# The first attention block by 64-key tiles in eight steps, and the second x tile normalised on Pool

## The chip, the cores and the metric

The kernel runs on one core of a Trainium2 chip. The metric is the device time of one execution in microseconds (us). The core has a matrix engine (TensorE, PE in the profile, its weight loads PEld), VectorE (DVE), ScalarE (ACT), GpSimd (Pool) and a queue engine that issues transfers (SyncE, SP). Each runs its own instructions in the order in which they stand, and waits for the others by semaphores. Matrix results land in PSUM, here in banks of 128 x 512 float32; in this kernel VectorE and ScalarE move them on, never Pool.

## What is computed

S = 2048 rows, D = 448 columns, 16 heads of 28, a window W of 256 keys, a feed-forward width F = 1792. The two branches read the same normalised x, and everything is summed:

```python
q, k, v = qkv[0], qkv[1], qkv[2]          # xn @ wqkv
scores = jnp.einsum("bhqd,bhkd->bhqk", q, k) * (Dh ** -0.5)
mask = (idx[:, None] - idx[None, :] >= 0) & (idx[:, None] - idx[None, :] < W)
p = _softmax(jnp.where(mask[None, None], scores, -1e9), axis=-1)
A = (p @ v) @ wo
B = (_gelu(xn @ w_gate) * (xn @ w_up)) @ w_down
return x + A + B                           # xn = _layernorm(x)
```

## The kernel before

**Blocks.** The rows are worked in four blocks of 512 (`qb`). Each block has an attention stage, a gate stage (gate and up projections, Gelu, product) and a down projection that runs as filler in the next block's attention. One block's attention is a fixed list of score steps (`steps_of`): each step fills one PSUM tile `sc` of 128 keys x 4 heads x 512 columns (four banks), ScalarE takes its exponential into an SBUF tile `p_sb` (L688), the entries outside the window are zeroed, and later `pv` multiplies with V. There is only one `sc` tile in the attention stage, so a step's matmuls wait for the exponential of the step before. Between two steps TensorE is given filler work by a table, `plan`: a tuple `(u, 2)` takes two pieces from generator `u`, a function is called at its place, and strings such as "sums" name small jobs.

**Groups.** The 16 heads are four groups `g` of four heads. Queries and keys of a group come from `qk_copies`, V from `v_copy`. In the first block groups 1 to 3 are projected during steps 0 to 2 (`gen_qk`), then come the up projections of five of the seven column pairs (`gen_up`, tile `ue`), then V and the first three groups of the second block (`gen_pairs`, generator `w`).

**First block, before.** Keys go by tiles of 128: nine steps (L570 to L580), each of 8 matmuls of 28 x 128 weights. Pool zeroes the entries outside the window (`masked`, L614). A group's product with V uses one PSUM bank; VectorE copies it to `oc` (L666).

**Other blocks.** Keys go by tiles of 64, so that two halves of TensorE's rows work on two key tiles at once: 16 or 24 matmuls a step. VectorE multiplies the edges by ready-made masks (`apply_masks`, L604, three products a step). A group's product with V uses two banks, one for each half; ScalarE copies the first to `oc` (L640) and VectorE adds the second (`add_halves`, L641).

**Banks.** Four banks, b0 to b3, serve all work but the scores; `take` hands out the one that was given back longest ago and `give` returns one. A bank is free only when the engine that empties it has got to that copy in its own order. In the first block the second up projection takes the banks of the third group's query and key, which ScalarE (L243) and VectorE (L244) empty.

**After the V product**, `sums` transposes `oc` and takes reciprocals (VectorE), `inverse` spreads them (VectorE), `scale_o` multiplies on Pool (L623).

**Start.** x tiles 0 to 3 each pass statistics (`stat`, VectorE), `rstd` (two small ScalarE operations), `norm` (VectorE, L170), four transposes on TensorE and a copy out of PSUM (L186). Tiles 0 and 2 use bank b2, 1 and 3 bank b3. Tiles 4 to 7 are normalised during steps 0 and 2 (L170 again, two operations each) and transposed by DMA.

**SP's order** around step 2: transposes of tiles 5 to 7, the half-swapped copies `xsw` of tiles 4 to 7 (L469), the half-swapped weights `wsq` (L475), which wait for Pool's pad copies (`fill_pads`, L283 and L285), then the gate weights and the rest.

Of the kernel before, what the change touches and what calls it, by code (L numbers as in the profile page):

```python
# [10 lines left out]
ALU = mybir.AluOpType  # L11
# [6 lines left out]
P = 128  # L18
# [9 lines left out]
def kernel(  # L28
# [11 lines left out]
    nc = tc.nc  # L40
# [123 lines left out]

    def norm(t):
        xn = work.tile([P, 4, P], bf16, name="xn", bufs=4)
        xf = xn[:, :, :].rearrange("p a b -> p (a b)")
        both = ((0, D, 0), (D, 64, 384))
        for lo, n, src in both if t > 3 else both[:1]:
            nc.vector.tensor_scalar(out=xf[:, lo:lo + n], in0=x_sb[:, t, src:src + n], scalar1=mv_all[:, t, 0:1],  # L170
                                    scalar2=rstd_all[:, t:t + 1], op0=ALU.subtract, op1=ALU.mult)
        xns[t] = xn
# [336 lines left out]
    def gated(qb, early, last_v, flush, hook):  # L509
# [11 lines left out]
        def gate(p):  # L521
            gt = phase[0].pool.tile([P, 2, QB], f32, name="gt", tag="s")
            for c in range(7):
                chunk([gt[:, i, :] for i in range(2)], wg, p, qb, c)
            if not p:
                last_v()
            ges[p] = work.tile([P, 4, QB], bf16, name="p_sb", bufs=5)[:, 0:2, :]
            nc.scalar.activation(out=ges[p][:, :, :], in_=gt[:, :, :], func=ACT.Gelu_apprx_tanh)  # L528

        def end(p):  # L530
# [28 lines left out]
    def steps_of(qb):  # L559
# [6 lines left out]
        if not qb:  # L566
            def four(g):
                return [(g, None, 3, 384, 128, 0), (g, None, 0, 0, 384, 128)], 512, [(None, (0,), 2 * P, True), (None, (384,), P, False)]

            for g in (0, 2):  # L570
                yield four(g)
                if not g:
                    yield [(0, None, 1, 128, 384, 0), (0, None, 2, 256, 128, 384)], 512, [(None, (0, 384), P, True), (None, (256,), P, False)]
                    yield [(0, None, 2, 384, 128, 0), (1, None, 0, 0, 384, 128)], 512, [(None, (128,), P, True), (None, (384,), P, False)]
                    yield [(1, None, 3, 384, 128, 0), (1, None, 1, 128, 384, 128)], 512, [(None, (0,), 2 * P, True), (None, (384,), P, False)]
                    yield [(1, None, 2, 256, 256, 0), (2, None, 2, 256, 256, 256)], 512, [(None, (0, 256), P, True)]
                else:
                    yield [(2, None, 1, 128, 384, 0), (3, None, 3, 384, 128, 384)], 512, [(None, (0, 384), P, True), (None, (256,), P, False)]
                    yield [(3, None, 0, 0, 384, 0), (3, None, 2, 384, 128, 384)], 512, [(None, (0,), P, True), (None, (256,), P, False)]
                    yield [(3, None, 1, 128, 384, 0), (3, None, 2, 256, 128, 384)], 512, [(None, (0, 384), P, True), (None, (256,), P, False)]  # L580
            return
# [23 lines left out]

    def masked(p_sb, half, cols, w, diag):
        r = slice(0, P) if half is None else slice(64 * half, 64 * half + 64)
        for c in cols:
            reg = p_sb[r, :, c:c + w]
            mid = [[0, 4]]  # L610
            if w > P:
                reg = reg.rearrange("p h (b q) -> p h b q", q=P)
                mid.append([0, w // P])
            nc.gpsimd.affine_select(out=reg, in_=reg, pattern=mid + [[1 if diag else -1, min(w, P)]], compare_op=ALU.is_ge, fill=0.0,  # L614
                                    base=0 if diag else -1, channel_multiplier=-1 if diag else 1)

    def attention(qb, plan):
# [21 lines left out]
        def add_halves(oc, ov):  # L639
            nc.scalar.copy(out=oc[:, :], in_=ov[0][:, :])  # L640
            nc.vector.tensor_tensor(out=oc[:, :], in0=oc[:, :], in1=ov[1][:, :], op=ALU.add)  # L641
            give(*ov)
# [5 lines left out]
        def pv(g):  # L648

            ov = [take("ov") for _ in range(2 if qb else 1)]  # L650
            todo = parts.pop(g)
            for n, (half, kt, q0, nq, col, p_sb) in enumerate(todo):
                k0 = 64 * half if half else 0
                r = slice(k0, k0 + (P if half is None else 64))
                for j in range(4):
                    nc.tensor.matmul(ov[half or 0][32 * j:32 * j + 32, q0:q0 + nq], lhsT=v_sb[r, kt, 4 * g + j, :],  # L656
                                     rhs=p_sb[r, j, col:col + nq], start=n == (half or 0), stop=n + len(ov) >= len(todo),
                                     tile_position=(k0, 32 * j), skip_group_check=True)
            oc = work.tile([P, QB], f32, name="oc", tag="wb" if g % 2 else "wa", bufs=1)
            if qb:  # L660
                if g > 2:
                    behind.append((oc, ov))
                else:
# [8 lines left out]
        for i, (scores, ncol, edges) in enumerate(steps):  # L672
# [7 lines left out]
            for g, half, kt, q0, nq, col in scores:  # L680
                k0, nk = (64 * half, 64) if half is not None else (0, P)
                for j in range(4):
# [3 lines left out]
                                     tile_position=(32 * j, k0), skip_group_check=True)  # L686
                parts.setdefault(g, []).append((half, kt, q0, nq, col, p_sb))
            nc.scalar.activation(out=p_sb[:, :, 0:ncol], in_=ss[:, :, 0:ncol], func=ACT.Exp, scale=SCALE)  # L688
# [24 lines left out]
        def rest():  # L713
            while fresh:
                apply_masks(*fresh.pop(0))
            while later:
                scale_o(*later.pop(0))
            pv(2)
            pv(3)

        def after(f):
            if qb == NB - 1:
                if inverses:
# [41 lines left out]
    norm(2)  # L765
    transp(2, nc.scalar.copy, "b2")
# [45 lines left out]
    def ahead3():  # L812
# [19 lines left out]
    for qb in range(NB):  # L832
# [226 lines left out]
```

## Time and profile before

| what | value |
|---|---|
| median of 3 runs | 212.53 us (212.52 to 212.82) |
| the profiled execution | 212.69 us |
| its span in the profile | 210.8 us |
| granted TensorE clock over the span | full |
| first score step begins (PE) | 11.2 us |
| first gate matmul of block 0 (PE) | 37.15 us |
| first score step of block 1 (PE) | 51.9 us |

A row of the chain of waits has a start, a length and what ran. A row of the timeline has a start and a length (of all merged instructions, with xcount), the engine, the line, the operation and its output and inputs; in brackets the idle time before it and what ended that. A row of the costliest groups has busy time and mean length in ns of one, then the idle time before. Lines are those of the kernel before.

### The profile page before, as it was taken

The page shows a single profiled execution, that of the slowest core. Times are in us where ns is not written, and L with a number is a line of the kernel's source. Part 1 is how long each engine was busy: PE and PEld are TensorE (multiplying, and loading weights), DVE is VectorE, ACT ScalarE, POOL GpSimd, SP SyncE. Part 2 cuts the span into 40 slices and gives each one's busy share as a digit, 9 for nine tenths or more (in the row PEclk, how much of TensorE's full clock was granted, in tenths as well). Part 3 has the DMA queues.
Part 4 walks back from the last instruction along what each step waited for, and adds up shares of the span by engine and source line. Part 5 has one row for each costly group of instructions (what it writes and reads, how often), then busy time and mean ns, then how long its engine had stood idle before and what let it go on. Part 6 is the DMA issues. An engine that isn't in the chain of part 4 may idle for free.

```text
span 210.8 us, 6335 instructions
## 1 busy us (share of the span) xinstructions
PE 205.1 (97%) x2678; PEld 96.5 (46%) x2682; DVE 157.8 (75%) x356; ACT 132.0 (63%) x124; POOL 48.4 (23%) x83
## 2 busy tenths in 40 slices
PE   7899999999999999999999999999999999999994
PEld 2333444444444445444445444544444454544562
DVE  6899998999788985696438897395385699659722
ACT  4699588566777977413778788523587787757000
POOL 5388658451000220040000112013000022005100
PEclk9999999999999999999999999999999999999999
DMA  6999989959411001003421000100100010100011
GB/s 176 275 223 230 107 215 220 218 175 234 110 48 48 22 5 39 7 3 71 75 75 47 25 0 27 23 0 15 32 3 0 5 47 0 48 3 0 22 59 41
DMA packets 24889, 15.67 MB, mean 74 GB/s; under 512 B 9208, under 2 KB 24728, under 8 KB 24856
## 3 DMA queue, kind: packets, MB, share of 16 engines
q1 hardware_dynamic: 23814, 14.87, 31.7%
q8 instruction: 22, 0.36, 0.7%
q10 hardware_dynamic: 1042, 0.34, 0.6%
q14 instruction: 11, 0.09, 0.1%
HBM read 9.26 MB, written 2.41 MB: 55 GB/s over the span
## 4 chain that ended last, share of the span: by engine, by line
PE 94%; DVE 2%; ACT 1%; DMA 1%; issue 1%; DVEq 0%; ACTq 0%
PE po L394 24%; PE gt L488 20%; PE u L488 12%; PE ue L488 8%; PE sc L684 7%; PE pq L333 7%; PE ov L656 5%; PE pv L319 4%; PE pq L190 2%; PE pl L394 2%; DVE st L155 1%; PE po L403 1%; DMA x_sb<-in_A_x_dram 1%; PE pv L190 1%; ACT p_sb L688 1%; PE s L190 1%
## 5 line engine op out<-in xcount | busy, mean ns | idle before, releaser
L688 ACT ACTIVATE p_sb<-sc 128x2048 bf16<-128x2048 f32 x39 | 73.2, 1878 | 20.0 <-PE sc L684 14.0
L528 ACT ACTIVATE p_sb<-gt 128x1024 bf16<-128x1024 f32 x28 | 28.7, 1025 | 33.6 <-PE gt L488 30.7
L623 POOL TENSOR_TENSOR oN<-oc,l 128x512 bf16<-128x512 f32 x16 | 21.9, 1374 | 117.9 <-DVE l L636 117.9
L488 PE MATMUL gt<-xnT,wg 64*128 64x512 bf16 x224 | 45.6, 376 | 0.0
L394 PE MATMUL po<-wd,hT 128*128 128x448 bf16 x210 | 43.3, 353 | 0.0
L488 PE MATMUL gt<-xsw,wg 64*128 64x512 bf16 x168 | 40.7, 376 | 0.0
L536 DVE TENSOR_TENSOR hT<-p_sb,u 128x512 bf16<-128x512 bf16 x34 | 21.9, 677 | 15.9 <-PE u L488 15.7
L604 DVE TENSOR_TENSOR p_sb<-p_sb,masks 128x256 bf16<-128x256 bf16 (+1 forms) x90 | 27.9, 365 | 7.5 <-ACT p_sb L688 7.5
L394 PEld LDWEIGHTS <-hT 128*128 128x128 bf16 x238 | 21.8, 98 | 19.5 <-issue 2.4
L488 PEld LDWEIGHTS <-wg 64*128 64x128 bf16 x392 | 19.0, 94 | 22.5 <-issue 0.2
L488 PEld LDWEIGHTS <-wu 64*128 64x128 bf16 x392 | 18.7, 94 | 22.5 <-issue 0.8
L488 PE MATMUL u<-xnT,wu 64*128 64x512 bf16 x136 | 28.1, 376 | 0.0
L488 PE MATMUL u<-xsw,wu 64*128 64x512 bf16 x102 | 24.7, 376 | 0.0
L488 PE MATMUL ue<-xnT,wu 64*128 64x512 bf16 x88 | 18.0, 377 | 0.0
L684 PE MATMUL sc<-qT,kT 28*64 28x320 bf16 (+7 forms) x648 | 16.4, 261 | 0.1
L488 PE MATMUL ue<-xsw,wu 64*128 64x512 bf16 x66 | 16.4, 377 | 0.0
L614 POOL TENSOR_SCALAR_AFFINE_SELECT p_sb<-p_sb 128x512 bf16<-128x512 bf16 (+1 forms) x21 | 14.2, 703 | 6.0 <-ACT p_sb L688 5.9
L641 DVE TENSOR_TENSOR oc<-oc,ov 128x512 f32<-128x512 f32 x12 | 8.2, 681 | 9.1 <-ACT oc L640 9.0
L684 PEld LDWEIGHTS <-kT 28*64 28x64 bf16 (+1 forms) x648 | 7.5, 102 | 13.3 <-issue 12.0
L382 DVE TENSOR_TENSOR res<-po,x_sb 128x448 bf16<-128x448 f32 x13 | 7.7, 621 | 7.7 <-PE po L403 4.4
L505 DVE CAST hT<-ue 128x512 bf16<-128x512 f32 x17 | 11.0, 678 | 1.3 <-PE ue L488 1.2
L170 DVE TENSOR_SCALAR xn<-x_sb,mv_all,rstd_all 128x448 bf16<-128x448 bf16 (+1 forms) x28 | 11.0, 434 | 0.3 <-ACT rstd_all L161 0.3
(111 smaller groups left out, 281.2 us busy)
## 6 DMA issues: line engine op xcount, KB each, us to landing
out_dram<-res SPq DMA_DIRECT2D x15, 112.0 KB
wd<-in_B_w_down_dram SPq DMA_DIRECT2D x2, 784.0 KB
x_sb<-in_A_x_dram SPq DMA_DIRECT2D x3, 448.0 KB
xsw<-xnT SPq DMA_DIRECT2D x6, 192.0 KB
wu<-in_B_w_up_dram SPq DMA_DIRECT2D x4, 224.0 KB
wg<-in_B_w_gate_dram SPq DMA_DIRECT2D x2, 448.0 KB
wu<-in_B_w_up_dram SPq DMA_DIRECT2D x2, 336.0 KB
wg<-in_B_w_gate_dram SPq DMA_DIRECT2D x2, 336.0 KB
```

The costliest lines, as they stand in the source:

```text
L170: nc.vector.tensor_scalar(out=xf[:, lo:lo + n], in0=x_sb[:, t, src:src + n], scalar1=mv_all[:, t, 0:1], scalar2=rstd_all[:, t:t + 1], op0= ...
L333: nc.tensor.matmul(ps, lhsT=w.rearrange("p h d -> p (h d)"), rhs=xchunk(qb, hi, c, qb * QB, QB), start=c == 0, stop=c == 6, tile_position= ...
L394: nc.tensor.matmul(po[:, 0:w], lhsT=x[:, k, tt * P:(tt + 1) * P], rhs=wt[:, k, lo:up], start=start and n == 0, stop=stop and n == len(term ...
L488: nc.tensor.matmul(ps, lhsT=w[64 * hi:64 * hi + 64, c, p * P:(p + 1) * P], rhs=xchunk(qb, hi, c, qb * QB, QB), start=c == 0, stop=c == 6, ...
L505: copy(out=hTs[qb][:, p + 7 * i, :], in_=us[i])
L528: nc.scalar.activation(out=ges[p][:, :, :], in_=gt[:, :, :], func=ACT.Gelu_apprx_tanh)
L536: nc.vector.tensor_tensor(out=hT[:, p + 7 * i, :], in0=ge[:, i, :], in1=u, op=ALU.mult)
L604: nc.vector.tensor_tensor(out=reg, in0=reg, in1=m, op=ALU.mult)
L614: nc.gpsimd.affine_select(out=reg, in_=reg, pattern=mid + [[1 if diag else -1, min(w, P)]], compare_op=ALU.is_ge, fill=0.0, base=0 if diag ...
L623: nc.gpsimd.tensor_tensor(out=oN[:, g, :], in0=oc[:, :], in1=inv, op=ALU.mult)
L684: nc.tensor.matmul(ss[k0:k0 + nk, j, col:col + nq], lhsT=kT[r, g, kt * P + k0:kt * P + k0 + nk], rhs=qT[r, g, ring(qb).start + q0:ring(qb) ...
L688: nc.scalar.activation(out=p_sb[:, :, 0:ncol], in_=ss[:, :, 0:ncol], func=ACT.Exp, scale=SCALE)
```

## The change

The first block takes the form of the others, with 64-key tiles, in eight steps (two for each group) instead of nine:

```diff
-            for g in (0, 2):
-                yield four(g)
...
+            for g in range(4):
+                yield [(g, 0, 0, 0, 320, 0), (g, 1, 0, 64, 320, 0), (g, 0, 2, 256, 192, 320), (g, 1, 2, 320, 192, 320)], 512, 1
+                yield [(g, 0, 1, 128, 320, 0), (g, 1, 1, 192, 320, 0), (g, 0, 3, 384, 128, 320), (g, 1, 3, 448, 64, 320),
+                       (g, 0, 2, 448, 64, 448), (g, None, 3, 384, 128, 384)], 512, 1
```

A tuple is group, half, key tile, first query, number of queries, column. The last one of the second step (half `None`) only fills columns that the exponential reads. Masks: the first four steps (groups 0 and 1) have six selects each on Pool, the last four have two mask products each on VectorE.

```diff
-    def apply_masks(p_sb, i):
+    def apply_masks(p_sb, i, n):
...
-        for js in ((0,), (1, 2), (3,)):
+        for js in ((0,), (1, 2), (3,))[0:n]:
...
+    def masked(p_sb):
+        for hi in range(2):
+            reg = p_sb[64 * hi:64 * hi + 64].rearrange("p h (b q) -> p h b q", q=64)
+            for part, kind in ((reg[:, :, 0], 1), (reg[:, :, 5], 1), (reg[:, :, 4], -1)):
+                nc.gpsimd.affine_select(out=part, in_=part, pattern=[[0, 4], [kind, 64]], compare_op=ALU.is_ge, fill=0.0, base=min(kind, 0),
+                                        channel_multiplier=-kind)
...
-            if qb:
-                fresh.append((p_sb, edges))
+            if qb or i > 3:
+                fresh.append((p_sb, edges, 3 if qb else 2))
             else:
-                for m in edges:
-                    masked(p_sb, *m)
+                masked(p_sb)
```

The V products of the first block use two banks, and ScalarE and VectorE share the way out; the last group's is flushed after the first Gelu:

```diff
+            q0 = 0 if qb else 64
+            nc.vector.tensor_tensor(out=oc[:, q0:], in0=oc[:, q0:], in1=ov[1][:, q0:], op=ALU.add)
...
-            ov = [take("ov") for _ in range(2 if qb else 1)]
+            ov = [take("ov") for _ in range(2)]
...
-            if qb:
-                if g > 2:
-                    behind.append((oc, ov))
-                else:
-                    add_halves(oc, ov)
+            if g > 2:
+                behind.append((oc, ov))
             else:
-                nc.vector.tensor_copy(out=oc[:, :], in_=ov[0][:, :])
-                give(*ov)
+                add_halves(oc, ov)
...
             nc.scalar.activation(out=ges[p][:, :, :], in_=gt[:, :, :], func=ACT.Gelu_apprx_tanh)
+            if not qb:
+                flush()
```

Copies out of PSUM change engines, and the first block's table is cut to eight steps:

```diff
-                v_copy(t + i, two[i], nc.vector.tensor_copy if i or not t % 4 or qb == 1 else nc.scalar.copy)
+                v_copy(t + i, two[i], nc.scalar.copy if (i if qb == 1 else t % 4 and not i) else nc.vector.tensor_copy)
...
-            qk_copies(qb, g, *two, nc.vector.tensor_copy if (g != 1) == (qb == 1) else nc.scalar.copy)
+            qk_copies(qb, g, *two, nc.vector.tensor_copy if g == (qb != 1) else nc.scalar.copy)
...
-            u = chain(gen_qk((1, 2, 3), {1: (3, pvs[3]), 2: (2, pvs[2])}), gen_up(0, (1, 2, 3, 0, 4), (3, 4)))
+            u = chain(gen_qk((1, 2, 3), {1: (3, pvs[3]), 2: (2, pvs[2])}), gen_up(0, (1, 2, 3, 0, 4), (2, 3, 4)))
...
-                    [lambda: spare.append(spare.pop(1)), (u, 2), ahead3, (u, 4)], [lambda: stat(8), (u, 11)],
-                    [lambda: stat(9), (u, 7), lambda: stat(10), (u, 7), lambda: fill_pads(True)], ["sums", (u, 7)],
-                    ["inverse", "scale", (w, 11)], [(w, 10)],
-                    [lambda: stat(11), (w, 7), lambda: rstd(8, 4), "sums", "inverse", (w, 7)]]
+                    [lambda: spare.append(spare.pop(1)), (u, 2), ahead3, (u, 4)], [(u, 11), lambda: stat(8)],
+                    [lambda: stat(9), (u, 12), lambda: fill_pads(True)], [(u, 9), "sums"],
+                    [(w, 7), "inverse", "scale", (w, 7), lambda: stat(10), (w, 3)],
+                    [(w, 4), lambda: stat(11), lambda: rstd(8, 4), (w, 7), "masks", "sums", (w, 7), "inverse"]]
```

The start: tile 1 goes to Pool, tile 0 is transposed and copied before the statistics of tiles 2 and 3, and tile 1's copy goes to VectorE. On SP the swapped weights go ahead of the second pair of swapped tiles:

```diff
     norm(0)
+    norm(1, nc.gpsimd)
+    transp(0, nc.scalar.copy, "b2")
     stat(2)
     rstd(2, 1)
-    transp(0, nc.scalar.copy, "b2")
-    norm(1)
     stat(3)
     rstd(3, 1)
     warmup(1)
-    transp(1, nc.scalar.copy, "b3")
+    norm(2)
+    transp(1, nc.vector.tensor_copy, "b3")
     pvs = [take("pv", D)]
     v_dense(0, pvs[0])
-    norm(2)
...
         swap(1, 4, 2)
-        swap(1, 6, 2)
         fill_pads(False)
         swap_weights()
+        swap(1, 6, 2)
```

Left out here: the wiring of halves in `pv` and of the filler tuple in the step loop, the removed helpers, a `sums()` between the last two V products, and the first block's inverses and sums, which now all run in the first call of `after`.

**Order, first place: ScalarE at the start**, from tile 1's `rstd` to the weight copy `wkp`. `lnv` rows are tile statistics, `tp` the transposed tile in PSUM. Before:

```order
L161 ACTIVATE rstd_all_127<-lnv_150 128x1
L160 ACTIVATE lnv_158<-mv_all_126,eps_t_106 128x1
L161 ACTIVATE rstd_all_127<-lnv_158 128x1
L186 COPY xnT_120<-tp_161 128x4x128
L160 ACTIVATE lnv_172<-mv_all_126,eps_t_106 128x1
L161 ACTIVATE rstd_all_127<-lnv_172 128x1
L186 COPY xnT_120<-tp_177 128x4x128
L186 COPY xnT_120<-tp_189 128x4x128
```

Now:

```order
L161 ACTIVATE rstd_all_127<-lnv_150 128x1
L186 COPY xnT_120<-tp_157 128x4x128
L160 ACTIVATE lnv_166<-mv_all_126,eps_t_106 128x1
L161 ACTIVATE rstd_all_127<-lnv_166 128x1
L160 ACTIVATE lnv_172<-mv_all_126,eps_t_106 128x1
L161 ACTIVATE rstd_all_127<-lnv_172 128x1
L186 COPY xnT_120<-tp_189 128x4x128
```

Tile 0's copy moved ahead of both later statistics, and one copy left ScalarE.

**Second place: Pool from the start to step 3**, as a difference (lines that differ only in number stand twice):

```order
-L770 COPY xnT<-xnT 64x512
+L170 TENSOR_SCALAR xn<-x_sb,mv_all,rstd_all 128x448
+L764 COPY xnT<-xnT 64x512
 L117 AFFINE_SELECT masks<-masks 64x64 x18
-L614 AFFINE_SELECT p_sb<-p_sb 128x4x256
-L614 AFFINE_SELECT p_sb<-p_sb 128x4x128 x6
+L602 AFFINE_SELECT p_sb<-p_sb 64x4x64 x18
 L283 COPY wqp<-wraw 128x4x4
 L285 COPY wqp<-wraw 128x12x4
```

Tile 1's normalisation came in at the front; seven selects of 512 or 1024 elements in a partition became eighteen of 256 ahead of the pad copies.

**Third place: VectorE in the last steps of the first block**, from the V copies of block 1 (`pv`) over its first groups' query and key copies (`pq`, `pk`) to the second group's. Before:

```order
L636 STREAM_TRANSPOSE l1_564<-inv_all_128 128x512
L226 CAST v_sb_76<-pv_620 128x16x28
L226 CAST v_sb_76<-pv_621 128x16x28
L226 CAST v_sb_76<-pv_638 128x16x28
L226 CAST v_sb_76<-pv_639 128x16x28
L243 CAST qT_124<-pq_669 128x512
L244 CAST kT_125<-pk_670 128x512
L155 BN_STATS st_701<-x_sb_74 128x6
L156 BN_AGGR mv_all_126<-st_701 128x2
L244 CAST kT_125<-pk_705 128x512
```

Now:

```order
L226 CAST v_sb_76<-pv_747 128x16x28
L624 STREAM_TRANSPOSE l1_682<-inv_all_128 128x512
L226 CAST v_sb_76<-pv_767 128x16x28
L155 BN_STATS st_785<-x_sb_74 128x6
L156 BN_AGGR mv_all_126<-st_785 128x2
L596 TENSOR_TENSOR p_sb_729<-p_sb_729,masks_105 128x4x64
L596 TENSOR_TENSOR p_sb_729<-p_sb_729,masks_105 128x4x128
L243 CAST qT_124<-pq_788 128x512
L244 CAST kT_125<-pk_789 128x512
L155 BN_STATS st_835<-x_sb_74 128x6
L156 BN_AGGR mv_all_126<-st_835 128x2
L244 CAST kT_125<-pk_842 128x512
```

Two of the four V copies went to ScalarE; a tile's statistics and a pair of mask products now stand ahead of the first group's copies.

More of the change, by code (lines that the diff above doesn't have):

```diff
@@ L163, with norm @@
     xns = {}
-    def norm(t):
+    def norm(t, eng=nc.vector):
         xn = work.tile([P, 4, P], bf16, name="xn", bufs=4)
@@ L169, in norm @@
         for lo, n, src in both if t > 3 else both[:1]:
-            nc.vector.tensor_scalar(out=xf[:, lo:lo + n], in0=x_sb[:, t, src:src + n], scalar1=mv_all[:, t, 0:1],
+            eng.tensor_scalar(out=xf[:, lo:lo + n], in0=x_sb[:, t, src:src + n], scalar1=mv_all[:, t, 0:1],
                                     scalar2=rstd_all[:, t:t + 1], op0=ALU.subtract, op1=ALU.mult)
@@ L604, in apply_masks @@
             nc.vector.tensor_tensor(out=reg, in0=reg, in1=m, op=ALU.mult)
[L606 to L615, printed above, removed]
+    def masked(p_sb):
[4 more added lines that the diff above has]
+                                        channel_multiplier=-kind)
     def attention(qb, plan):
@@ L648, in pv @@
         def pv(g):
-            ov = [take("ov") for _ in range(2 if qb else 1)]
+            ov = [take("ov") for _ in range(2)]
             todo = parts.pop(g)
             for n, (half, kt, q0, nq, col, p_sb) in enumerate(todo):
-                k0 = 64 * half if half else 0
-                r = slice(k0, k0 + (P if half is None else 64))
+                k0 = 64 * half
+                r = slice(k0, k0 + 64)
                 for j in range(4):
-                    nc.tensor.matmul(ov[half or 0][32 * j:32 * j + 32, q0:q0 + nq], lhsT=v_sb[r, kt, 4 * g + j, :],
-                                     rhs=p_sb[r, j, col:col + nq], start=n == (half or 0), stop=n + len(ov) >= len(todo),
+                    nc.tensor.matmul(ov[half][32 * j:32 * j + 32, q0:q0 + nq], lhsT=v_sb[r, kt, 4 * g + j, :],
+                                     rhs=p_sb[r, j, col:col + nq], start=n == half, stop=n + 2 >= len(todo),
                                      tile_position=(k0, 32 * j), skip_group_check=True)
             oc = work.tile([P, QB], f32, name="oc", tag="wb" if g % 2 else "wa", bufs=1)
-            if qb:
-                if g > 2:
-                    behind.append((oc, ov))
-                else:
-                    add_halves(oc, ov)
-            else:
-                nc.vector.tensor_copy(out=oc[:, :], in_=ov[0][:, :])
-                give(*ov)
+            if g > 2:
+                behind.append((oc, ov))
+            else:
+                add_halves(oc, ov)
             copied.append((g, oc))
@@ L680, in attention @@
             for g, half, kt, q0, nq, col in scores:
-                k0, nk = (64 * half, 64) if half is not None else (0, P)
+                fills = half is None
+                half = 1 if fills else half
+                k0, nk = 64 * half, 64
                 for j in range(4):
@@ L686, in attention @@
                                      tile_position=(32 * j, k0), skip_group_check=True)
-                parts.setdefault(g, []).append((half, kt, q0, nq, col, p_sb))
+                if not fills:
+                    parts.setdefault(g, []).append((half, kt, q0, nq, col, p_sb))
             nc.scalar.activation(out=p_sb[:, :, 0:ncol], in_=ss[:, :, 0:ncol], func=ACT.Exp, scale=SCALE)
             flush()
-            if qb:
-                fresh.append((p_sb, edges))
-            else:
-                for m in edges:
-                    masked(p_sb, *m)
+            if qb or i > 3:
+                fresh.append((p_sb, edges, 3 if qb else 2))
+            else:
+                masked(p_sb)
             while later:
@@ L718, in rest @@
             pv(2)
+            if not qb:
+                sums()
             pv(3)
         def after(f):
+            while not qb and not f and (copied or inverses):
+                if inverses:
+                    inverse()
+                if copied:
+                    sums()
             if qb == NB - 1:
```

11 lines of the change are left out of this document (removed).

## The prediction

> **What bounds the kernel now.** I read the page first: busy shares and the chain that ended last.
>
> ```profile
> span 210.8 us, 6335 instructions
> ...
> PE 205.1 (97%) x2678; PEld 96.5 (46%) x2682; DVE 157.8 (75%) x356; ACT 132.0 (63%) x124; POOL 48.4 (23%) x83
> ...
> PE 94%; DVE 2%; ACT 1%; DMA 1%; issue 1%; DVEq 0%; ACTq 0%
> ```
>
> TensorE is 94% of that chain, so a change pays by fewer TensorE microseconds, or by an earlier start, and costs wherever it makes TensorE wait. Next the chain in order of time (start, length, what), first the start:
>
> ```profile
> 5.59 0.28 DVE xn L170
> 5.88 0.55 DVE st L155
> 6.67 0.30 ACT lnv L160
> 7.19 0.48 ACT xnT L186
> 7.72 0.38 PE tp L185 x4
> 8.10 0.57 PE pv L190 x3
> 8.67 1.42 PE s L190 x6
> ```
>
> Until 7.7 us VectorE sets the pace, with one normalisation (tile 1) between two statistics; then ScalarE's copy of tile 1, which frees the bank that tile 3's transposes need. From 8.1 on it is TensorE. The same view for the first block and, for 64-key steps, the second:
>
> ```profile
> 11.73 1.89 ACT p_sb L688
> ...
> 19.57 2.48 PE ue L488 x22
> 22.05 0.61 PE ov L656 x20
> 22.65 0.33 PE sc L684 x8
> 22.98 3.13 PE ue L488 x28
> ...
> 28.06 0.60 PE ov L656 x16
> ...
> 38.66 1.10 PE ov L656 x36
> ...
> 47.42 1.51 PE u L488 x14
> ...
> 57.90 0.35 PE sc L684 x16
> ...
> 62.60 0.68 PE ov L656 x40
> ...
> 81.60 1.26 PE ov L656 x81
> ```
>
> The exponential at 11.73 holds up the second score step, since one score tile serves all steps; after it the chain stays on TensorE through the block.
>
> **The change, part by part.** *Score steps.* 14 matmuls take 1.51 (47.42), so 28 should take 3.02; the row 22.98 has 3.13, so leaving a score step costs 0.11. A 128-key step thus costs 0.33 + 0.11 = 0.44, nine of them 3.96. A 64-key step has 0.35 (57.90); its exit is not shown apart, and I take 0.12, so eight cost 3.76: **-0.20** (bounds: -0.28 with the same exit, -0.04 with 0.14).
>
> *Probability times V.* Before: 0.61 + 0.60 + 1.10 = 2.31. The second block's 64-key form has 1280 columns in each half, here at most 1024; a column is 1.51/7/512 = 0.42 ns, so 256 fewer save 0.11: twice 0.68 - 0.11, and 1.26 - 0.22 for the last two, 2.18 in all: **-0.13**.
>
> *The start.* Rows for the order on ScalarE and VectorE, and the nearest rows for a TensorScalar on Pool, which the trace does not have:
>
> ```profile
> 4.85 0.39 PE L185 MATMUL tp<-ident,xn 128*128 128x128 bf16 x4
> 6.06 0.57 ACT L186 COPY xnT<-tp 128x512 bf16<-128x512 bf16 x1
> L770 POOL COPY xnT<-xnT 64x512 bf16<-64x512 bf16 x1 | 0.6, 607 | 5.1 <-ACT wkp L743 5.1
> L623 POOL TENSOR_TENSOR oN<-oc,l 128x512 bf16<-128x512 f32 x16 | 21.9, 1374 | 117.9 <-DVE l L636 117.9
> ```
>
> Tile 0's copy moves from 6.06 to about 5.3 (its transposes end at 4.85 + 0.39), so the two pairs of small ScalarE operations for tiles 2 and 3 (0.50 each: 6.67 to 7.19 with gaps) end at 6.97 in place of 7.19. VectorE loses 0.28 of chain; it normalises tile 2 at 6.45, copies tile 1 at 6.75, and normalises tile 3 at 7.1, ready at 7.5 where tile 3's transposes began at 7.72. That is **-0.20** for the projections at 8.67. Pool's normalisation starts at about 5.05; it lies between 0.55 (a one-input copy, by 448/512) and 1.2 (a two-input product); I take 0.6. Tile 1 is copied at 6.75 if Pool needs under 1.2, so either end leaves the sum alone.
>
> [...]
>
> *Masks on Pool.* The first four steps now have six selects of 64x4x64 each, where Pool had two or three larger ones.
>
> ```profile
> L117 POOL TENSOR_SCALAR_AFFINE_SELECT masks<-masks 64x64 bf16<-64x64 bf16 x18 | 4.3, 244 | 0.8
> L614 POOL TENSOR_SCALAR_AFFINE_SELECT p_sb<-p_sb 128x512 bf16<-128x512 bf16 x18 | 11.0, 637 | 4.3 <-ACT p_sb L688 4.3
> 9.41 5.05 POOL L117 TENSOR_SCALAR_AFFINE_SELECT masks<-masks 64x64 bf16<-64x64 bf16 x18
> 17.50 0.64 DVE L170 TENSOR_SCALAR xn<-x_sb,mv_all,rstd_all 128x448 bf16<-128x448 bf16 x1
> 17.37 0.64 POOL L614 TENSOR_SCALAR_AFFINE_SELECT p_sb<-p_sb 128x512 bf16<-128x512 bf16 x1
> L170 DVE TENSOR_SCALAR xn<-x_sb,mv_all,rstd_all x3: 290/384/385, 18.3 to 18.8; 128x448 bf16<-128x448 bf16 x2, 128x64 bf16<-128x64 bf16 x1
> 17.50 2.19 DVE L170 TENSOR_SCALAR xn<-x_sb,mv_all,rstd_all 128x448 bf16<-128x448 bf16 x6
> 19.08 0.61 DVE L170 TENSOR_SCALAR xn<-x_sb,mv_all,rstd_all 128x64 bf16<-128x64 bf16 x1
> 19.60 0.68 DVE L244 CAST kT<-pk 128x512 bf16<-128x512 f32 x1
> ```
>
> For 256 elements between 64 (244 ns) and 512 (637) a straight line gives 0.41, so 18 selects run without a pause from about 14.3 to 21.7. That matters to VectorE. A normalisation that takes 0.384 alone took 0.64 when it met a select (17.37 to 18.01) and ended 0.13 after it; the one at 19.08 took 0.61 for 0.29. Pool's pause around 18.5 let the rest through. Without it each of the six waits out a select: 0.38 (its spacing) + 0.13 for a wide one, + 0.04 for a narrow one, 2.8 in all, less about 0.2 for the first: 2.6, where it was 2.19 (bounds: 1.5, all six without a wait, and 4.0, the same plus six whole selects). Behind them on VectorE stands the third group's key copy (19.60), whose bank the second up-projection takes: eight matmuls into the row at 19.57, at 20.5, now 20.4. Normalisations from 17.35 end at 19.95, the copy at 20.55: TensorE waits **+0.20** where it had 0.2 to spare.
>
> [...]
>
> *Other work.* ScalarE loses an exponential and a transposition copy and gains four output copies, an up-projection copy, two V copies and a query copy; VectorE trades four copies for four adds, and eight mask products for five instructions that left it or shrank.
>
> ```profile
> L640 ACT COPY oc<-ov 128x512 f32<-128x512 f32 x12 | 7.0, 584 | 3.2 <-PE ov L656 3.2
> 60.24 0.83 DVE L604 TENSOR_TENSOR p_sb<-p_sb,masks 128x256 bf16<-128x256 bf16 x3 [0.48 <-ACT p_sb L688]
> 41.48 1.02 ACT L528 ACTIVATE p_sb<-gt 128x1024 bf16<-128x1024 f32 x1 [1.46 <-PE gt L488]
> ```
>
> On ScalarE step 4 is tightest: two 0.58 copies, then 1.89, ending near 25.0, where TensorE's next scores come at 25.5. On VectorE a pair of masks is about 0.55 of the 0.83 for three. Following its list (third order excerpt above), the first key group's two copies end near 35.0 and the third group's matmuls want those banks at 35.2: covered by 0.2. In the gate stage ScalarE now has output copy, Gelu, output copy, Gelu. The second copy waits for Pool's product of group 1 (1.37, from about 39.1), and behind it stand the second Gelu and, for its bank, the fourth gate: 40.5 + 0.58 + 1.02 makes 42.2, asked for at 42.45. I cost all three at nothing; each microsecond beyond its cover is one on TensorE.
>
> *Transfers.* SP now puts the swapped weights before the second pair of swapped tiles, which so leaves 1.2 later and is read by the second V pair near 30.3.
>
> ```profile
> 23.55 2.62 SPq L469 DMA_DIRECT2D xsw<-xnT  x4
> ...
> 26.27 0.56 SPq L475 DMA_DIRECT2D wsq<-wqp  x1
> 21.43 0.22 POOL L285 COPY wkp<-wraw 128x48 bf16<-128x48 bf16 x1
> ```
>
> It is issued by 27.4, 2.9 before its use. The weights wait for Pool's pad copies, now behind 18 selects: 21.7, some 0.6 for the meetings with VectorE, and nine copies of 0.22 at most make 24.3, and SP arrives about 24.8. If Pool comes later, everything behind on SP slips with it, the second swapped pair and the gate weights first. When a transfer lands, no row shows; I cost this at nothing, and 2.9 us is the point from which it would cost.
>
> **Sum**: -0.20 - 0.13 - 0.20 + 0.20 = -0.33. The profiled execution is 212.69, so 212.36; the median of the runs is 0.16 below it: **212.2**. What decides 0.2% is 0.43 us, about what a measurement of this kernel can tell from no change.
>
> **The rivals.** *The wait does not come* (TensorE saves all of 0.53): 212.0, down to 211.7 if steps leave as cheaply as before. [...] Against: the two rows above.
>
> *Pool holds VectorE longer* (the slow side). At the 4.0 end the normalisations last to 21.35, the key copy to 21.95, TensorE waits 1.55: net +1.0, 213.5. Point of decision: slower than before once the six last over 2.9.
>
> *VectorE becomes the bound behind step 6.* If its list is 0.5 later, the third key group waits 0.3 for banks and the last V product 0.2 for its own: 212.7. For it: stands at 0.2 of cover on a chain of sixteen instructions. Against: before it had about as much to do.
>
> *Selects cost what 512 elements cost*, 0.64: 24 of them and the pad copies (2.0 at most) from 14.3 end near 31.7, and the second V product, due about 27.9, waits 3.8: 216. The 244 ns row speaks against it.
>
> **Chances.** Forecast 0.34 (own range 211.9 to 212.5), no wait 0.30, long hold 0.16, VectorE bound 0.14, dear selects 0.06. Faster: 0.27 of the no-wait case and a third of the forecast, 0.38. Slower: 0.14 of the long hold, 0.04 of the VectorE case and the dear selects, 0.24. Within 0.2%: the rest, 0.38. Range 211.6 to 213.3: the low end is no wait with every term at its better bound, the high end reaches most of the long hold.
>
> **What would show it.** In the profile after: projections near 8.45; score steps of 0.35 with exits near 0.12; the V products near 0.57; six normalisations near 17.35 of about 2.6 and a TensorE gap of about 0.2 at 20.4; selects of about 410 ns; first gate matmuls near 36.8 rather than 37.15. A gap over 0.6 at 20.4, or one before 35.2 or 28, would make it wrong, and so would a difference that arises after 52 us.

## The result, and the profile after

The changed kernel takes 213.00 us (median of 22 runs, 212.77 to 214.99), the kernel before beside it 212.70 us (22 runs, 212.51 to 213.12). The medians differ by 0.30 us (0.14%), where 212.2 was forecast. Five of the 22 runs lie apart from the rest, at 213.94 to 214.99; the recorded ratio weighs them too (the means differ by 0.57 us) and is 1.0027, with a 95% interval of 1.0017 to 1.0037, clear of no change.

| what | before | after |
|---|---|---|
| profiled execution, us | 212.69 | 212.89 |
| its span, us | 210.8 | 211.1 |
| projections begin (PE), us | 8.67 | 9.16 |
| first score step begins (PE), us | 11.27 | 11.76 |
| first gate matmul of block 0, us | 37.15 | 37.46 |
| row of 14 up-projection matmuls, us | 47.42 | 47.62 |

The chain of waits of the changed kernel (start, length, what), first the start, then the first block. Line numbers up to L488 are those of before; the later ones shown here are 6 to 13 lower: L645 is the V product, L671 the scores, L676 the exponential.

```profile
4.42 0.30 ACT lnv L160
4.75 0.21 ACT rstd_all L161
...
5.05 1.87 POOL xn L170
...
6.97 0.40 PE tp L185 x4
7.37 0.57 PE pv L190 x3
7.94 0.24 PE tp L185 x4
8.19 0.40 PE tp L185 x4
8.59 0.57 PE pv L190 x3
9.16 1.42 PE s L190 x6
...
11.76 0.42 PE sc L671 x16
...
12.27 1.89 ACT p_sb L676
...
20.17 2.58 PE ue L488 x22
22.75 0.55 PE ov L645 x32
23.30 0.35 PE sc L671 x16
23.65 2.70 PE ue L488 x24
...
28.75 0.55 PE ov L645 x32
...
37.46 1.51 PE gt L488 x14
38.97 0.99 PE ov L645 x59
...
47.62 1.51 PE u L488 x14
```

Pool's normalisation now stands in the chain, and with 1.87 us it is its longest piece there between the first statistics and the projections. These begin 0.49 us later than before. From there to the row at 47.62 the changed kernel takes 38.46 us where the kernel before took 47.42 - 8.67 = 38.75, so the attention part wins 0.29. The two leave +0.20, which is the difference of the profiled executions, and nothing is added behind.

The timeline of the changed kernel's start (start, length, engine, line, operation; in brackets idle time and what ended it):

```profile
5.05 1.86 POOL L170 TENSOR_SCALAR xn<-x_sb,mv_all,rstd_all 128x448 bf16<-128x448 bf16 x1 [1.42 <-ACT rstd_all L161]
5.22 0.63 PE L185 MATMUL tp<-ident,xn 128*128 128x128 bf16 x4
...
5.89 0.59 ACT L186 COPY xnT<-tp 128x512 bf16<-128x512 bf16 x1 [0.94 <-PE tp L185]
...
6.93 0.40 DVE L170 TENSOR_SCALAR xn<-x_sb,mv_all,rstd_all 128x448 bf16<-128x448 bf16 x1 [0.68 <-ACT rstd_all L161]
...
6.97 0.40 PE L185 MATMUL tp<-ident,xn 128*128 128x128 bf16 x4 [0.74 <-POOL xn L170]
...
7.41 0.42 DVE L186 COPY xnT<-tp 128x512 bf16<-128x512 bf16 x1
```

Two things are late at one point. TensorE stands idle for 0.74 us until Pool has tile 1, and VectorE copies it at 7.41. And tile 0's transposes take 0.63 us where the profile before showed 0.39: TensorE is slower there (the nine dummy matmuls of 512 columns ahead of them take 4.02 us, 0.45 each; three matmuls of that width take 0.65 later on, 0.22 each, about half). So ScalarE's copy of tile 0 starts at 5.89 instead of 5.3, the small operations behind it are late, and VectorE normalises tile 2 only at 6.93. By these rows either alone puts tile 1's copy at about 7.3 or later: the normalisation ends at 7.33, the transposes at 7.37.

### The profile page after: what moved, and what is told of

Read it like the earlier page. It is cut to its first block, busy times and chain, and to the rows that moved or that the text cites. A ratio compares the mean times of both kernels' runs of the same rounds, so it can differ in the third digit from the quotient of the medians.

```text
span 211.1 us, 6670 instructions
## 1 busy us (share of the span) xinstructions
PE 205.8 (98%) x2842; PEld 99.0 (47%) x2842; DVE 157.4 (75%) x360; ACT 133.8 (63%) x130; POOL 45.8 (22%) x87
## 4 chain that ended last, share of the span: by engine, by line
PE 94%; ACT 1%; DMA 1%; DVE 1%; POOL 1%; issue 0%; DVEq 0%; ACTq 0%
PE po L394 24%; PE gt L488 20%; PE u L488 12%; PE ue L488 8%; PE sc L671 6%; PE pq L333 6%; PE ov L645 5%; PE pv L319 4%; PE pq L190 2%; PE pl L394 2%; PE pv L190 1%; PE po L403 1%; DMA x_sb<-in_A_x_dram 1%; ACT p_sb L676 1%; POOL xn L170 1%; PE s L190 1%
## 5 line engine op out<-in xcount | busy, mean ns | idle before, releaser
L676 ACT ACTIVATE p_sb<-sc 128x2048 bf16<-128x2048 f32 x38 | 71.4, 1878 | 17.3 <-PE sc L671 12.4
L611 POOL TENSOR_TENSOR oN<-oc,l 128x512 bf16<-128x512 f32 x16 | 21.4, 1346 | 127.5 <-DVE l L624 127.5
L488 PE MATMUL gt<-xnT,wg 64*128 64x512 bf16 x224 | 45.6, 376 | 0.0
L488 PE MATMUL gt<-xsw,wg 64*128 64x512 bf16 x168 | 40.7, 376 | 0.0
L596 DVE TENSOR_TENSOR p_sb<-p_sb,masks 128x256 bf16<-128x256 bf16 (+1 forms) x98 | 30.6, 366 | 7.5 <-ACT p_sb L676 7.5
L488 PEld LDWEIGHTS <-wg 64*128 64x128 bf16 x392 | 19.1, 94 | 22.3
L488 PEld LDWEIGHTS <-wu 64*128 64x128 bf16 x392 | 19.1, 94 | 21.9 <-issue 0.6
L488 PE MATMUL u<-xnT,wu 64*128 64x512 bf16 x136 | 28.1, 376 | 0.0
L488 PE MATMUL u<-xsw,wu 64*128 64x512 bf16 x102 | 24.7, 376 | 0.0
L488 PE MATMUL ue<-xnT,wu 64*128 64x512 bf16 x88 | 18.0, 377 | 0.0
L630 DVE TENSOR_TENSOR oc<-oc,ov 128x512 f32<-128x512 f32 (+1 forms) x16 | 10.5, 657 | 9.8 <-ACT oc L628 9.6
L488 PE MATMUL ue<-xsw,wu 64*128 64x512 bf16 x66 | 16.4, 377 | 0.0
L671 PE MATMUL sc<-qT,kT 28*64 28x320 bf16 (+4 forms) x736 | 16.2, 259 | 0.1
L671 PEld LDWEIGHTS <-kT 28*64 28x64 bf16 x736 | 8.2, 103 | 12.7 <-issue 10.9
L628 ACT COPY oc<-ov 128x512 f32<-128x512 f32 x16 | 9.4, 585 | 3.6 <-PE ov L645 3.6
```

Source lines behind the costliest of these rows:

```text
L488: nc.tensor.matmul(ps, lhsT=w[64 * hi:64 * hi + 64, c, p * P:(p + 1) * P], rhs=xchunk(qb, hi, c, qb * QB, QB), start=c == 0, stop=c == 6, ...
L596: nc.vector.tensor_tensor(out=reg, in0=reg, in1=m, op=ALU.mult)
L611: nc.gpsimd.tensor_tensor(out=oN[:, g, :], in0=oc[:, :], in1=inv, op=ALU.mult)
L671: nc.tensor.matmul(ss[k0:k0 + nk, j, col:col + nq], lhsT=kT[r, g, kt * P + k0:kt * P + k0 + nk], rhs=qT[r, g, ring(qb).start + q0:ring(qb) ...
```

## The experiments

The kernels ran in three sets, each on one chip with the kernel before beside it (medians 212.67, 212.75 and 212.73). Changes in us are differences of medians; the ratios are those on record, which weigh the late runs too.

**The two halves apart.** The first kernel is the kernel before with the changed start alone, the second the changed kernel with the old start (the core of its diff):

```diff
     norm(0)
-    norm(1, nc.gpsimd)
-    transp(0, nc.scalar.copy, "b2")
     stat(2)
     rstd(2, 1)
+    transp(0, nc.scalar.copy, "b2")
+    norm(1)
     stat(3)
     rstd(3, 1)
     warmup(1)
-    norm(2)
-    transp(1, nc.vector.tensor_copy, "b3")
+    transp(1, nc.scalar.copy, "b3")
...
+    norm(2)
```

> The kernel before with the changed start alone: tile 1 normalised by Pool, tile 0's copy ahead of the small ScalarE operations for tiles 2 and 3, tile 1 copied by VectorE. Theory (the start is what was lost): projections near 9.16 in place of 8.67, end about +0.5 us against the kernel before (213.2), and some runs at 214 or over, since the stretch in which TensorE waits for Pool is here too. Rival 1 (the start is worth what was forecast and the loss came in from elsewhere): -0.2. Rival 2 (the start's delay is taken up later): within 0.1 of before.

> The changed kernel with the start of the kernel before. Theory (start +0.5, the rest as forecast): projections at 8.67 again, -0.2 to -0.4 us against the kernel before (212.3 to 212.5), no run over 213.5. Rival 1 (the loss is in the attention part): +0.1 to +0.3. Rival 2 (the runs at 214 and over come from the transfers, which the attention part orders): such runs stay, about one in four.

The start alone: 213.24 against 212.67, ratio 1.0032 (1.0014 to 1.0049), +0.57 us, one of 9 runs at 214.71; projections at 9.21. The rest alone: 212.37, ratio 0.9985 (0.9976 to 0.9994), -0.30 us, the highest of 11 runs 212.97. Together +0.27, where the whole change came to +0.30: the halves add up, and the loss is all in the start. (The profiled execution of the second kernel took 212.78, with the projections at 8.94, 0.27 later than in the kernel before; why they are later there is not shown.)

**What in the start.** Tile 1's normalisation back on VectorE, all else as changed:

```diff
-    norm(1, nc.gpsimd)
+    norm(1)
```

> The changed kernel with tile 1's normalisation on VectorE, at the same place of the program; nothing else. Theory P (Pool's 1.86 us is the whole of the start's loss): the normalisation ends near 5.2, TensorE's 0.74 us of waiting goes, -0.4 us or more against the changed kernel (212.6 or less). Theory C (the loss is tile 0's copy, which stands ahead of the small ScalarE operations and is late where TensorE still runs at half rate at 5.2 us): VectorE's list is as late as before, the projections start within 0.1 of 9.16, same time as the changed kernel (213.0). Where P and C are both needed, it lies between.

212.53 us: 0.47 below the changed kernel's 213.00 (from the set above, with the kernel before at 212.70), the side of theory P, and still 0.16 above the version with the old start. Its timeline:

```profile
5.05 0.40 DVE L170 TENSOR_SCALAR xn<-x_sb,mv_all,rstd_all 128x448 bf16<-128x448 bf16 x1 [0.28 <-ACT rstd_all L161]
5.23 0.63 PE L185 MATMUL tp<-ident,xn 128*128 128x128 bf16 x4
5.36 0.62 DVE L155 BATCH_NORM_STATS2 st<-x_sb 128x6 f32<-128x448 bf16 x1
...
5.90 0.59 ACT L186 COPY xnT<-tp 128x512 bf16<-128x512 bf16 x1 [0.89 <-PE tp L185]
...
7.26 0.42 DVE L186 COPY xnT<-tp 128x512 bf16<-128x512 bf16 x1
...
7.59 0.39 DVE L170 TENSOR_SCALAR xn<-x_sb,mv_all,rstd_all 128x448 bf16<-128x448 bf16 x1
```

The tile is ready at 5.45 instead of 6.91, but VectorE's copy of it comes only 0.15 us earlier. Tile 0's transposes are as slow and ScalarE's copy as late (5.90) as in the changed kernel; the chain of waits, however, does not lead over them:

```profile
5.05 0.40 DVE xn L170
5.44 0.55 DVE st L155
...
6.20 0.52 DVE st L155
...
7.26 0.42 DVE xnT L186
7.68 0.32 DVE xn L170
```

From 5.05 to 8.0 it stays on VectorE, which now has tile 1 ahead of the statistics of tiles 2 and 3. Those of tile 3 stand at 6.20 in this chain and at 5.88 in that of the kernel before, 0.32 later, and the projections begin 0.33 later (9.00 against 8.67). So what this kernel still loses is lost by VectorE's list. The profiled executions, 212.53 and 212.89, differ by 0.24 in the trace up to the row at 47.62: the projections begin at 9.00, 0.16 earlier, and the up-projection row of 2.58 is 2.50 here (0.08); the rest lies behind that row and around the span.

The other way round, ScalarE's old order with Pool kept:

```diff
     norm(1, nc.gpsimd)
-    transp(0, nc.scalar.copy, "b2")
     stat(2)
     rstd(2, 1)
+    transp(0, nc.scalar.copy, "b2")
```

> The changed kernel with tile 0's copy on ScalarE behind tile 2's pair of small operations again, as before; Pool still normalises tile 1. Theory P (Pool alone already sets the start: tile 1's transposes wait for it until 6.97, VectorE copies at 7.4 and normalises tile 3 at 7.75): tile 2's normalisation comes earlier but the projections stay near 9.16, time as the changed kernel, 213.0. Theory C (the copy ahead of the small operations counts by itself): -0.15 us, 212.85.

212.96 us, ratio to before 1.0010 (0.9990 to 1.0029): as the changed kernel, theory P. VectorE now has tile 2 at 6.23 and then waits 0.98 us for tile 1, which Pool, 0.17 us later in this execution, ends at 7.08; the projections begin at 9.33. So with Pool normalising, ScalarE's order makes no difference here (212.96 against 213.00): Pool alone sets the end of the start.

A try at a better start, VectorE's copy of tile 1 moved into the stretch where VectorE waits for ScalarE:

```diff
-    norm(1, nc.gpsimd)
+    norm(1)
...
-    norm(2)
     transp(1, nc.vector.tensor_copy, "b3")
+    norm(2)
```

> The changed kernel with tile 1's normalisation on VectorE, and VectorE's copy of tile 1 ahead of tile 2's normalisation, in the stretch in which VectorE waits for ScalarE. From the profile with the normalisation on VectorE, where the projections start at 9.00: the copy ends near 7.2, the normalisations of tiles 2 and 3 near 7.9, projections at 8.9, 212.4. If the copy comes at 7.0 or later, because it holds back the statistics' successors instead, 212.5 or more. The version with the start of before stands at 212.37.

A miss: 212.79, ratio 1.0000 (0.9983 to 1.0018). The copy does start earlier, at 6.85, but the normalisations of tiles 2 and 3 then follow back to back until 7.93, and the projections begin at 8.96, only 0.04 earlier: VectorE's list is the limit here too.

**What Pool's normalisation costs by itself.** The version with the old start, with Pool instructions whose results nobody reads: one in the start, twelve late, where Pool has nothing to do. (One run only, 212.56 us; its time is not compared.)

```diff
+            if (qb, f) == (2, 6):
+                xn = work.tile([P, 4, P], bf16, name="xn", bufs=4)
+                probe(0, (0, 1, 2, 3) * 3, xn[:, :, :].rearrange("p a b -> p (a b)")[:, 0:D])
```

> The changed kernel with the start of before, and TensorScalar instructions on Pool whose results nobody reads: one like the change's beside VectorE's statistics in the start, and late, in a stretch in which Pool has nothing to do, three each of: two operations with a scalar from memory for each partition, one operation with such a scalar, two operations with constants, and a copy; all 128x448 bf16. Theory 1 (the 1.86 us are the operation's own price): near 1.86 in both places, and less for the lighter forms, down to about 0.55 for the copy. Theory 2 (VectorE beside it makes it long): near 1.86 in the start and 0.6 to 1.2 late.

Its Pool timeline, the one in the start and five of the late ones:

```profile
5.15 1.86 POOL L747 TENSOR_SCALAR wsq<-x_sb,mv_all,rstd_all 128x448 bf16<-128x448 bf16 x1 [1.51 <-ACT rstd_all L161]
...
148.57 1.86 POOL L747 TENSOR_SCALAR xn<-x_sb,mv_all,rstd_all 128x448 bf16<-128x448 bf16 x1
150.53 1.41 POOL L749 TENSOR_SCALAR xn<-x_sb,rstd_all 128x448 bf16<-128x448 bf16 x1
152.02 1.72 POOL L751 TENSOR_SCALAR xn<-x_sb 128x448 bf16<-128x448 bf16 x1
153.81 0.56 POOL L753 COPY xn<-x_sb 128x448 bf16<-128x448 bf16 x1
...
160.43 2.22 POOL L747 TENSOR_SCALAR xn<-x_sb,mv_all,rstd_all 128x448 bf16<-128x448 bf16 x1
```

The price is the operation's own: 1.86 in the start and in two of the three late ones. The third late one took 2.22; it began beside VectorE's mask products (0.83 us from 160.25 on). One operation with a scalar per partition takes 1.41, two with constants 1.72, a copy 0.56. So of the 1.86 most goes with the two arithmetic operations (1.72 against the copy's 0.56), and little with the scalars from memory (1.86 against 1.72).

**The runs at 214.** TensorE's idle stretch in the start made shorter by one dummy matmul, and longer by taking the present one out:

```diff
-    warmup(1)
+    warmup(2)
```

```diff
-    warmup(1)
```

> The changed kernel with one more dummy matmul of 512 columns in the stretch in which TensorE waits for Pool. Theory A (the runs at 214 and over are those in which TensorE stays at half rate after its idle stretch): the median stays at 213.0 and no run comes over 213.6. Rival B (they come from a late transfer): median 213.0, and about one run in four still over 213.8.

> The changed kernel without the dummy matmul ahead of tile 1's transposes, so that TensorE stands idle from about 5.85 to 6.97 us while Pool normalises (0.74 us before). Theory A (the runs at 214 and over are those in which TensorE stays at half rate after the idle stretch): they become more frequent, half of the runs or more at 213.8 and over, against 5 of 22; in such a run's profile 512 columns take near 0.6 us for some 3 us behind the stretch. Rival B (a late transfer): one in four or fewer, and the median as in the changed kernel, 213.0.

Shorter: 212.92 (212.74 to 213.39), none of 11 runs over 213.6 (at the changed kernel's 8 of 34, counting its repeat below, that would come by chance about once in 19). Longer: 213.69 (212.85 to 214.42), 6 of 12 runs at 214.02 and over, and the profiled execution is one of them, at 214.02. Its chain of waits, then its timeline:

```profile
5.24 1.87 POOL xn L170
...
7.16 0.61 PE tp L185 x4
7.77 1.12 PE pv L190 x3
8.89 0.85 PE tp L185 x8
9.74 0.86 PE pv L190 x3
10.61 1.29 PE s L190 x6
...
13.09 0.42 PE sc L671 x16
```

```profile
7.16 0.61 PE L185 MATMUL tp<-ident,xn 128*128 128x128 bf16 x4 [1.31 <-POOL xn L170]
...
10.44 0.81 PE L190 MATMUL s<-xnT,wqp 128*128 128x512 bf16 x3
```

After 1.31 us of idling the same three matmuls for V take 1.12 us (0.37 for 448 columns, less than the 0.6 for 512 that was expected) where the changed kernel's chain has 0.57, and four transposes 0.61 where it has 0.40; the projections take what they took before again (0.81 for three). The first score step begins at 13.09 instead of 11.76, +1.33, of which 0.19 is a later start of Pool; the six late runs lie about as far from the other six (212.85 to 213.35). Over all kernels, by the length of the stretch in which TensorE waits for Pool: none, 0 of 68 runs at 213.8 and over; 0.43 us, 0 of 11; 0.74 to 0.98 us, 10 of 55 (8 of 34 at 0.74, 2 of 21 at 0.87 and 0.98); 1.31 us, 6 of 12. Theory A fits this, but only one of these 16 late runs was profiled. Five of the 16 have a mean granted clock of 0.990 to 0.992, all other runs of these kernels 0.998 to 1.000; 0.9% of 211 us would be 1.9 us (an estimate), so for these five a lower granted clock is a rival that no trace settles. The one profiled has 0.998. In the kernel before, which idles twice for less than 0.5 us there, one run of a group of 29 came to 214.70 (granted clock 0.990), and the highest of another group of 35 was 213.82.

**Once more on one chip, and SP's order.** The changed kernel, the version with the old start and the one with the normalisation on VectorE were repeated side by side; the fourth is the version with the old start and SP's old order.

```diff
         swap(1, 4, 2)
+        swap(1, 6, 2)
         fill_pads(False)
         swap_weights()
-        swap(1, 6, 2)
```

> The changed kernel once more, on the same chip as the next three, so that the parts can be subtracted without a chip between them. Theory (start +0.57, attention -0.30, together additive): 213.0, and one run in four or five at 213.8 and over.

> The changed kernel with the start of the kernel before, a second time. Theory: -0.3 us against the kernel before (ratio 0.9985) and -0.6 against the changed kernel, no run at 213.8 and over. If the first time was the chip's doing: within 0.1 of before.

> The changed kernel with tile 1's normalisation on VectorE, a second time. Theory (Pool's duration is the larger part of the start's loss, the new order of the copies the rest): -0.4 us against the changed kernel, and +0.1 to +0.2 against the version with the start of before. If order alone were harmless: the same as that version.

> The version with the start of before, and on SP the second pair of swapped tiles ahead of the swapped weights again. Forecast's reading (both orders are early enough): same as the version with the start of before, within 0.1. Rival (the new order saves or costs a wait on the second V pair or the gate weights): 0.2 or more away from it.

| kernel | median, us | runs | ratio to before (212.73) |
|---|---|---|---|
| changed | 213.07 (212.73 to 215.26) | 12 | 1.0033 (1.0011 to 1.0055) |
| old start | 212.46 (212.35 to 212.92) | 11 | 0.9991 (0.9982 to 1.0000) |
| changed, tile 1 on VectorE | 212.71 (212.52 to 212.97) | 11 | 0.9998 (0.9986 to 1.0009) |
| old start, SP's old order | 212.35 (212.21 to 213.43) | 12 | 0.9978 (0.9968 to 0.9987) |

Start as changed costs 0.61 here: Pool in VectorE's place 0.36 of it, the rest of the new start 0.25 (0.47 and 0.16 the first time). With SP's old order the median is 0.11 lower, between the forecast's 0.1 and the rival's 0.2; the two ranges overlap, and whether it is more than chance was not tried further. The attention change with the old start beats both kernels, by 0.30 and 0.27 us against before (the second interval touches no change), and by 0.38 with SP's old order as well.

## Why the prediction was wrong

**The start (forecast -0.20, came out at +0.49 in the profile, +0.57 by itself).** This term turned the sign. One step of it is shown to have failed, a second by rows only. The first: "it lies between 0.55 (a one-input copy, by 448/512) and 1.2 (a two-input product); I take 0.6. Tile 1 is copied at 6.75 if Pool needs under 1.2, so either end leaves the sum alone." Pool took 1.86, above the upper bound and beyond the point of decision, TensorE stood idle for 0.74 us behind it, and with VectorE in Pool's place 0.36 to 0.47 us came back. The bounds were wrong, since neither row was of the same kind of operation. The product of two tensors (1.2 for 448 columns, the prediction's estimate) was no upper bound for two operations in a row (1.86), and the cheap reading was in fact the copy's (0.56 in the runs).

The second step: "Tile 0's copy moves from 6.06 to about 5.3 (its transposes end at 4.85 + 0.39)". Both numbers were read from one execution, and its 0.39 did not hold in most others. Of the 14 profiles of this study, 12 show 0.62 or 0.63 for the same four transposes, from 5.21 or later on, and only two 0.39 or 0.40 (the kernel before, and the repeat of the version with the old start). The old order did not mind, because the copy stood behind tile 2's small operations: with the old start the projections' first row in the timeline is at 8.55 and 8.73 in two executions with the slow transposes (SP's old order, Pool's prices) and at 8.62 and 8.63 in the two with the quick ones. The new order puts the copy ahead, and in the changed kernel VectorE then waits 0.68 us for ScalarE before it normalises tile 2. So by the rows the -0.20 would not have come with a quick Pool either. No run shows this by itself: with Pool as slow as it is, ScalarE's order makes no difference (212.96), and where tile 1 is on VectorE the chain leads over VectorE's list, which costs the 0.16 to 0.25 that are left there.

**Score steps (-0.20) and V products (-0.13).** Right in mechanism, and near in size. In the chain after, 24 up-projection matmuls take 2.70; at 1.51/14 each that is 2.59, so leaving a step costs 0.11, and 0.12 by the next such row (18 matmuls in 2.06), where 0.12 was taken. The V products are 0.55 + 0.55 + 0.99 = 2.09 against 2.18 forecast and 2.31 before: -0.22.

**The wait on the third group's keys (+0.20).** Overestimated. First the timelines of VectorE and Pool in the changed kernel, then, from the chain of waits of its repeat, the up projections behind the third group's key copy:

```profile
18.06 2.38 DVE L170 TENSOR_SCALAR xn<-x_sb,mv_all,rstd_all 128x448 bf16<-128x448 bf16 x6
...
20.35 0.68 DVE L244 CAST kT<-pk 128x512 bf16<-128x512 f32 x1
...
14.99 7.36 POOL L602 TENSOR_SCALAR_AFFINE_SELECT p_sb<-p_sb 64x256 bf16<-64x256 bf16 x18
```

```profile
20.20 2.50 PE ue L488 x22
```

18 selects in 7.36 us are 0.41 each, as forecast, and they run without a pause. But the six normalisations took 2.38, not 2.6, and 2.07 in the repeat of the same kernel and in the versions with the old start, with tile 1 on VectorE, and with the shorter idle stretch. The up-projection row is 2.58 in this execution and 2.50 in the second: a wait of 0.08 in one and none in the other. The step that failed is "each of the six waits out a select". So the first rival, in which the wait does not come, is nearer to what happened here than the forecast is; its 212.0 did not come, since the start lost. By the forecast's own point of decision (2.9) the rival in which Pool holds VectorE longer did not come about; nor did VectorE as the bound behind step 6, or the dear selects. Selects grow longer as well: single ones beside normalisations took up to 0.54, against the 0.41 above, in the first execution of the version with the old start:

```profile
18.44 0.70 DVE L170 TENSOR_SCALAR xn<-x_sb,mv_all,rstd_all 128x448 bf16<-128x448 bf16 x2
18.56 0.54 POOL L602 TENSOR_SCALAR_AFFINE_SELECT p_sb<-p_sb 64x256 bf16<-64x256 bf16 x1
```

**What was costed at nothing** (step 4 on ScalarE, VectorE's list behind step 6, the gate stage, SP's order) cost nothing that shows. As measured, score steps (0.20) and V products (0.22) are worth 0.42; from the first score step to the row of 14 up-projection matmuls (11.27 to 47.42 before) the changed kernel wins 0.29 with the wait of 0.08, and 0.38 in its repeat without it (11.80 to 47.57), so 0.04 or 0.05 is all that is left over. By the medians the attention part alone is faster by 0.27 to 0.30.

So the forecast's sum of -0.33 was -0.13 for the attention with its wait and -0.20 for the start; measured apart, they are -0.30 and +0.57.

## What to carry to other kernels

Price an operation on another engine from a row of the same operation there, and where there is none, let the upper bound reach beyond the point at which the sum changes sign; here a copy (0.56) and a product of two tensors (1.2, an estimate from 1.37 for 512 columns) did not bound a TensorScalar on Pool (1.86). Four transposes in the first microseconds took 0.39 or 0.40 in two profiles and 0.62 or 0.63 in twelve, so read such a duration from several executions before anything is put behind it in a queue. And a step that lies beside other work in the start cost twice here: by the wait itself (TensorE idle for 0.74 us in the changed kernel, 1.31 without the dummy matmul), and, in the late execution that was profiled, by slower matmuls behind the wait (1.12 us for three where the changed kernel has 0.57).

## What the runs showed of the hardware

On Pool, one instruction over 128 x 448 bf16 took 0.56 us as a copy, 1.41 with one arithmetic operation and 1.86 with two and scalars per partition (2.22 once, beside VectorE's mask products); VectorE takes 0.40 for the last.

TensorE's slower matmuls in the first microseconds (0.45 us for a dummy matmul of 512 columns against 0.22 later, 0.63 for four transposes against 0.40) came to an end between about 4.2 and 10 us after the start, though the same nine dummy matmuls stand ahead in all. (The 4.2 is an estimate: the nine dummy matmuls took 3.49 us instead of 4.02 in one execution, so about the last two and a half ran in 0.22 each. So is the 10, from the late execution that was profiled: three matmuls for V still take 0.86 at 9.74, three of 512 columns 0.81 at 10.44.) The granted clock does not show it: the profiles of the kernel before and of the changed kernel give it as 1.00 from 1.4 to 5.4 us, over the slow dummy matmuls, as later. In the first execution with tile 1 on VectorE three matmuls took 1.10 from 6.54 on (0.74 in others) with no idle stretch before them. But late runs were most frequent behind the longest idle stretch, 6 of 12 behind 1.31 us, at a price of 1.1 to 1.4 us (1.33 less Pool's later start of 0.19 in the profile, up to 1.4 by the medians of late and other runs).

The same program showed both values: with the old start, tile 0's transposes took 0.40 in one execution and 0.63 in the other. What decides between them was not shown.
